# Converting float64 weights to float32: the absolute value scaled on ScalarE instead of a maximum on GpSimd or VectorE and a mask of bits

## The chip, the cores and the metric

The kernel runs on one core of a Trainium2 chip. The engines are named as in the profile: PE is TensorE (matmuls; PEld its weight loads), DVE is VectorE, ACT is ScalarE, POOL is GpSimd, SP is SyncE, from whose queue (SPq) nearly all DMA transfers are issued. The metric is the device time of one execution in microseconds; it is given as the median of several runs.

## The reference, cut to what matters

Eight batches of attention with eight heads, 576 positions, 64 values per head. The mask lets heads 0 to 3 see the 32 positions up to their own ("local") and heads 4 to 7 every 32nd position ("strided"). The output goes through a mix over positions of rank 32 and a feed-forward block. U, V, w_ch1 and w_ch2 arrive as float64.

```python
attn = softmax(where(mask, q @ k.T / 8, -1e9))         # per batch and head
x = concat_heads(attn @ v)                             # (8, 576, 512)
h = x.transpose(0, 2, 1) @ U @ V                       # rank 32
u = x + h.transpose(0, 2, 1)
out = u + np.maximum(u @ w_ch1, 0.0) @ w_ch2           # 512 -> 2048 -> 512
```

## The kernel before

The 4608 rows of u are worked through in 18 blocks of up to 256 rows. For each block `gemm1` (L625, sums in the PSUM tile `ph`) makes 128 of the 2048 hidden values at a time, and `gemm2` (L642, sums in `acc` or `px`) adds their share of the output. A float32 factor is held as two parts, hi and lo (`uh`/`ul`, `gh`/`gl`, `w[:, 0]`/`w[:, 1]`), and three products are made in place of one. Between the two products ACT makes `gh` (L629) and DVE makes `gl` (L630); a `gemm2` needs both, and each of them has three buffers.

The weights come in 32 chunks of 128 x 512. A chunk is loaded as 8-byte words (`raw`, L157, on SP's queue), converted to float32 in a tile `cv` by `to_f32` (L106 to L124), rounded to its hi part on ACT (L169) and subtracted from it on POOL for the lo part (L170). U and V go through `to_f32` too, as three smaller tiles. `to_f32` reads the high word of a float64 as if it were a float32, and its steps are:

- the absolute value on ACT (L115);
- the maximum with `TINY` (2 to the power -15), so that what is below float32's range does not wrap (L116). The argument `CMODE = (1, 1, 1, 0, 1, 1, 1, 0)` puts this step on POOL for three chunks of four and on DVE for the fourth; for U and V it is on DVE;
- a shift by three bits to the left together with an and-mask, on DVE (L118);
- an and/or with the high word on DVE, which brings back the sign and the top bit of the exponent (L120);
- a shift/or with the low word on DVE, for the last three bits (L122).

The first 90 us hold the attention of batch 0, staggered pair of heads by pair, its mix (L475 to L509, which makes u from x by way of `ta`, `tst` and V) and the transposes of the first blocks (L590 to L595); the conversions of the first chunks lie between them in the program. In that part a pair of heads goes through: transposes of q and k on PE (L203), copies of them out of PSUM on ACT into `kZ` and `qT` (L226), scores (L299), softmax (L322 to L325), a transpose of the weights (L330) and its copy `PT`, and the product with the values in `vt` or `vt_kept` (L340). `vt` and `vt_kept` hold the values twice, shifted by 32 rows; the second time is a copy on ACT (L226). Strided heads get their values by way of a DRAM tile `sd` and write their results `o_sb` to a DRAM tile `od`, from which they are loaded into `xg`, the tile of x.

After that the loop over blocks runs. Its first two blocks are worked through in turns, and the conversions of the remaining chunks lie between them, by the need of the next product or at 1.35 chunks for each step (`CONVM`). The attention of later batches fills the gaps of the later blocks.

The order on each engine's queue is not that of the program's text: the framework places each instruction by a modelled time line of its own, so that a change in an instruction's kind or count can move others. An engine runs its own queue strictly in that order.

Of the kernel before, what the change touches and what calls it, by code (L numbers as in the profile page):

```python
# [7 lines left out]
F32 = mybir.dt.float32  # L8
# [5 lines left out]
ALU = mybir.AluOpType  # L14
# [32 lines left out]
def fused_kernel(ctx, tc, q, k, v, U, V, w1_in, w2_in, masks, eye, out):  # L47
# [29 lines left out]
    banks = {"n": 0, "prefix": True}  # L77

    def psx2():
        """Two PSUM banks; those of the output sums serve too before the first of them."""  # L80
        banks["n"] += 1
        if banks["prefix"] and banks["n"] % 3 == 0:
            return ps_acc.tile([128, 2, 512], F32, name="acc")
        return ps_x.tile([128, 2, 512], F32, name="px")
# [18 lines left out]
    Vst = const.tile([96, S], F32R, name="Vst")  # L103
    raws, w_parts = {}, {}

    def to_f32(raw, p, n, eng=nc.vector, one=False):  # L106
        """float32 of float64 bits: the top 24 significant bits; below float32's range 0."""
        rv = raw.bitcast(I32).rearrange("p (n two) -> p n two", two=2)
        lo_w, hi_w = rv[:, 0:n, 0], rv[:, 0:n, 1]
        cv = att([128, 512], "cv")  # L110
        f = cv[0:p, 0:n]
        if one:
            eng.tensor_scalar(out=f, in0=hi_w.bitcast(F32), scalar1=TINY, scalar2=None, op0=ALU.abs_max)
        else:
            nc.scalar.activation(out=f, in_=hi_w.bitcast(F32), func=AF.Abs)  # L115
            eng.tensor_scalar(out=f, in0=f, scalar1=TINY, scalar2=None, op0=ALU.max)  # L116
        i = cv.bitcast(I32)[0:p, 0:n]
        nc.vector.tensor_scalar(out=i, in0=i, scalar1=3, scalar2=0x3FFFFFF8,  # L118
                                op0=ALU.logical_shift_left, op1=ALU.bitwise_and)
        nc.vector.scalar_tensor_tensor(out=i, in0=hi_w, scalar=-0x40000000, in1=i,  # L120
                                       op0=ALU.bitwise_and, op1=ALU.bitwise_or)
        nc.vector.scalar_tensor_tensor(out=i, in0=lo_w, scalar=29, in1=i,  # L122
                                       op0=ALU.logical_shift_right, op1=ALU.bitwise_or)
        return f  # L124
# [35 lines left out]
    def weights():  # L160
        for n, (i, g, t) in enumerate(chunks):
            while wl["n"] <= n:
                next(wl["gen"])
                wl["n"] += 1
            f = to_f32(raws[i, g, t], 128, 512, *((nc.vector, False), (nc.gpsimd, False), (nc.vector, True), (nc.gpsimd, True))[CMODE[n % 8]])
            parts = const.tile([128, 2, 512], F32R, name=f"w{i}_{g}_{t}", tag=f"w{i}_{g}_{t}")
            w_parts[i, g, t] = parts
            hi, lo = parts[:, 0], parts[:, 1]
            nc.scalar.copy(out=hi, in_=f)  # L169
            nc.gpsimd.tensor_tensor(out=lo, in0=f, in1=hi.bitcast(F32), op=ALU.subtract)  # L170
            yield
# [24 lines left out]
        return xn  # L196

    def transpose_natural(dsts, xn, strided, engines):
        """dst[d, position] per head of load_natural, the positions class by class when strided."""
        tp = psx2().rearrange("p a x -> p (a x)")  # L200
        for t in range(5):
            n = 128 if t < 4 else 64
# [30 lines left out]
    vts = []  # L233

    def acquire(names):
        """The first of these buffers that no other part of the program is filling or reading, when one is free."""
        while True:
            for name in names:
                if name not in held:
                    held[name] = True  # L240
                    return name
            yield

    def value_tiles():
        """Values of two heads, each in its half of the rows and of the columns; what stays is written once."""
        for vt in (big([128, NCH, 2, D + 1], "vt"), const.tile([128, NCH, 2, D + 1], F32, name="vt_kept")):
            nc.gpsimd.memset(vt, 0.0)
            for hh in range(2):
                nc.gpsimd.memset(vt[64 * hh:64 * hh + 64, :, hh, D:D + 1], 1.0)
            vts.append(vt)  # L250

    def attention_pair(b, pr, sd, od, last):
        """Two heads of a batch: 32 positions attend to themselves and to the 32 before, in the order of the
        positions (local heads) or class by class (strided heads)."""
        strided = pr >= 2
        early = b < NSP
        pi = 4 * b + pr if early else None
# [125 lines left out]
            yield  # L383

    def strided_heads(b):
        """The strided heads of a batch: partition (head, class), 18 positions in each class."""
        st = big([128, 2 * NCH * D], "st")
        sq, sk = (st[:, x * NCH * D:(x + 1) * NCH * D].rearrange("p (i d) -> p i d", d=D) for x in range(2))

# [76 lines left out]
        return xgs[b], tails[b // 2]  # L466

    def mix_t(b, half):
        """tst[:, half] = hi, lo, hi parts of U^T x."""
        xg, xt = x_tiles(b)  # L470
        tb = 64 * (b % 2)
        cs = slice(256 * half, 256 * half + 256)
# [103 lines left out]
    uT = {}  # L576

    def transposes(n):
        """Halves of u^T of a block: DVE transposes blocks of 32 x 32, DMA carries each to its quarter of the partitions."""
        def parts():  # L580
            uT[n] = [ubuf([128, 2, 4, NDC, 32], name, F32R) for name in ("uh", "ul")]
            return uT[n]
# [88 lines left out]
            counts["conv"] += 1  # L671

    def needed(item):
        """Chunks of weights for gemm1 of this block and part of FF, and for gemm2 of those before."""
        return len(chunks) if item[0] >= NLEAD else 8 * (item[1] // FPG) + 4 + item[1] % FPG

    gen, nb, done = None, 1, 0
# [107 lines left out]
```

## Time and profile before

| what | value |
|---|---|
| time, median of 3 runs | 1019.03 us (1016.57 to 1020.28) |
| span of the profiled execution, first to last instruction | 1016.9 us |
| PE busy | 958.7 us (94%) |
| DVE busy | 648.8 us (64%) |
| POOL busy | 406.1 us (40%) |
| ACT busy | 313.0 us (31%) |

The profiled execution has no time of its own beside its span; the span lies 2.1 us below the median of the runs and inside their range. Busy times are those in which an engine executes an instruction; starts are in microseconds from the first instruction.

### The profile page before, as it was taken

The page shows a single profiled execution, that of the slowest core. Times are in us where ns is not written, and L with a number is a line of the kernel's source. Part 1 is how long each engine was busy: PE and PEld are TensorE (multiplying, and loading weights), DVE is VectorE, ACT ScalarE, POOL GpSimd, SP SyncE. Part 2 cuts the span into 40 slices and gives each one's busy share as a digit, 9 for nine tenths or more (in the row PEclk, how much of TensorE's full clock was granted, in tenths as well). Part 3 has the DMA queues.
Part 4 walks back from the last instruction along what each step waited for, and adds up shares of the span by engine and source line. Part 5 has one row for each costly group of instructions (what it writes and reads, how often), then busy time and mean ns, then how long its engine had stood idle before and what let it go on. Part 6 is the DMA issues. An engine that isn't in the chain of part 4 may idle for free.

```text
span 1016.9 us, 18249 instructions
## 1 busy us (share of the span) xinstructions
PE 958.7 (94%) x7164; PEld 832.6 (82%) x7164; DVE 648.8 (64%) x1184; ACT 313.0 (31%) x691; POOL 406.1 (40%) x397
## 2 busy tenths in 40 slices
PE   4576889999999999999999999999999999999997
PEld 2345678898898889978889888988898889999996
DVE  3567998979786868634768686968686864312121
ACT  6777545213311241111422133123321242111110
POOL 1324966965383429201447353735383410000000
PEclk9797999999999999999999999999999999999999
DMA  7865913042523250401252425052514200101000
GB/s 189 221 164 143 366 39 67 2 109 48 91 42 68 48 90 22 88 1 42 47 91 43 68 47 91 21 89 48 91 39 71 47 22 21 42 1 43 1 21 21
DMA packets 186094, 71.33 MB, mean 70 GB/s; under 512 B 148952, under 2 KB 177272, under 8 KB 186008
## 3 DMA queue, kind: packets, MB, share of 16 engines
q1 hardware_dynamic: 186008, 70.16, 32.4%
q8 instruction: 56, 0.92, 0.4%
q14 instruction: 30, 0.25, 0.1%
HBM read 51.64 MB, written 11.80 MB: 62 GB/s over the span
## 4 chain that ended last, share of the span: by engine, by line
PE 76%; DVE 7%; SPq 5%; POOL 4%; issue 3%; DMA 3%; ACT 2%; DVEq 0%; POOLq 0%; ACTq 0%
PE ph L625 35%; PE acc L642 33%; SPq L94 4%; POOL tmp L409 3%; PE px L299 2%; PE px L340 1%; DVE cv L120 1%; DVE st L439 1%; PE px L330 1%; POOL w L170 1%; SPq L157 1%; DVE cv L122 1%; PE px L475 1%; DMA raw<-in_moe_w_ch_dram 1%; PE px L501 1%
## 5 line engine op out<-in xcount | busy, mean ns | idle before, releaser
L625 PE MATMUL ph<-uh,w 128*128 128x256 f32 x2304 | 472.6, 286 | 8.1 <-DVE gl L630 7.3
L625 PEld LDWEIGHTS ph<-uh,w 128*128 128x128 f32 x2304 | 379.3, 190 | 29.4 <-DVE gl L630 11.9
L642 PE MATMUL acc<-w,gh 128*128 128x512 f32 x1088 | 341.5, 393 | 0.0
L625 PE MATMUL ph<-ul,w 128*128 128x256 f32 x1152 | 331.5, 288 | 1.6 <-DVE ul L595 1.6
L630 DVE SCALAR_TENSOR_TENSOR gl<-ph,gh 128x256 fp32r<-128x256 f32 x288 | 120.6, 419 | 244.9 <-ACT gh L629 243.5
L629 ACT ACTIVATE gh<-ph 128x256 fp32r<-128x256 f32 x288 | 110.3, 384 | 504.9 <-PE ph L625 452.8
L437 POOL TENSOR_TENSOR tmp<-st,s_st 128x448 f32<-128x448 f32 (+7 forms) x162 | 144.2, 912 | 237.2 <-DVE st L439 148.7
L625 PEld LDWEIGHTS ph<-ul,w 128*128 128x128 f32 x1152 | 217.3, 189 | 11.4 <-DVE ul L595 1.8
L642 PEld LDWEIGHTS acc<-w,gh 128*128 128x128 f32 x1088 | 194.3, 188 | 31.2 <-issue 2.2
L642 PE MATMUL acc<-w,gl 128*128 128x512 f32 x544 | 213.2, 392 | 0.2 <-DVE gl L630 0.2
L409 POOL TENSOR_TENSOR tmp<-st 128x576 f32<-128x576 f32 (+6 forms) x162 | 169.4, 1089 | 74.9 <-DMA st<-in_k_dram 29.2
L439 DVE TENSOR_REDUCE st<-tmp 128x64 f32<-128x64 f32 (+8 forms) x162 | 138.3, 873 | 4.4 <-POOL tmp L437 3.4
L642 PEld LDWEIGHTS acc<-w,gl 128*128 128x128 f32 x544 | 102.2, 188 | 19.3 <-issue 1.1
L411 DVE TENSOR_REDUCE s_st<-tmp 128x9 f32<-128x576 f32 (+6 forms) x162 | 87.8, 564 | 14.2 <-POOL tmp L409 13.6
L170 POOL TENSOR_TENSOR w<-cv,w 128x512 fp32r<-128x512 f32 x32 | 45.3, 1424 | 49.1 <-ACT w L169 46.9
L116 POOL TENSOR_SCALAR cv<-cv 128x512 f32<-128x512 f32 x24 | 40.0, 1670 | 42.2 <-ACT cv L115 36.8
L454 ACT COPY xg<-st 32x256 f32<-32x256 f32 x96 | 38.7, 404 | 37.3 <-DVE st L439 36.4
L299 PE MATMUL px<-kZ,qT 128*32 128x128 f32 x612 | 30.5, 303 | 8.5 <-ACT qT L226 8.4
L299 PEld LDWEIGHTS px<-kZ,qT 128*32 128x32 f32 x612 | 20.4, 120 | 18.3 <-ACT qT L226 9.9
L169 ACT CAST w<-cv 128x512 fp32r<-128x512 f32 x32 | 19.7, 618 | 44.0 <-DVE cv L122 37.4
L612 DVE TENSOR_TENSOR ul<-u,uh 128x1024 fp32r<-128x1024 f32 x15 | 21.9, 1460 | 14.3 <-ACT uh L611 14.3
L120 DVE SCALAR_TENSOR_TENSOR cv<-raw,cv 128x512 int32<-128x512 int32 x32 | 28.3, 888 | 0.4
(123 smaller groups left out, 686.6 us busy)
## 6 DMA issues: line engine op xcount, KB each, us to landing
raw<-in_moe_w_ch_dram SPq DMA_DIRECT2D x32, 512.0 KB, 8.0
out_dram<-xg SPq DMA_DIRECT2D x32, 256.0 KB, 2.2
u<-bt SPq DMA_DIRECT2D x240, 32.0 KB, 1.9
vt_kept<-in_v_dram SPq DMA_DIRECT2D x28, 144.0 KB, 3.6
st<-in_q_dram SPq DMA_DIRECT2D x24, 144.0 KB, 3.4
st<-in_k_dram SPq DMA_DIRECT2D x24, 144.0 KB, 4.8
st<-in_v_dram SPq DMA_DIRECT2D x24, 144.0 KB, 3.2
xn<-in_k_dram SPq DMA_DIRECT2D x48, 72.0 KB, 2.4
```

The costliest lines, as they stand in the source:

```text
L94: last_dma[0] = nc.sync.dma_start(out=out, in_=in_).ins
L116: eng.tensor_scalar(out=f, in0=f, scalar1=TINY, scalar2=None, op0=ALU.max)
L170: nc.gpsimd.tensor_tensor(out=lo, in0=f, in1=hi.bitcast(F32), op=ALU.subtract)
L299: nc.tensor.matmul(sp[32 * c4:32 * c4 + 32, t], qT[:, 32 * c:32 * c + 32], kZ[:, :, 32 * c:32 * c + 64], start=not early, stop=True, skip_ ...
L409: nc.gpsimd.tensor_tensor(out=tmp[:, 0:n], in0=sk[:, j0:j0 + n], in1=sq[:, i:i + 1].broadcast_to([128, n, D]), op=ALU.mult)
L411: late.append(lambda tmp=tmp, n=n, i=i, j0=j0: nc.vector.tensor_reduce(out=s_st[:, i, j0:j0 + n], in_=tmp[:, 0:n], axis=AX.X, op=ALU.add))
L437: nc.gpsimd.tensor_tensor(out=tv, in0=sv[:, 0:i + 1, d0:d0 + step], in1=s_st[:, i, 0:i + 1].broadcast_to([128, i + 1, step]), op=ALU.mult)
L439: late.append(lambda tv=tv, i=i, d0=d0, step=step: nc.vector.tensor_reduce(out=o_st[:, i, d0:d0 + step], in_=tv.rearrange("p j d -> p d j" ...
L625: nc.tensor.matmul(ph[:, 0:W], w_parts[0, g, dc][:, part, fs], ut[:, :, :, dc, :], start=(dc == 0 and i == 0), stop=(dc == NDC - 1 and i = ...
L629: nc.scalar.activation(out=gh[:, 0:W], in_=ph[:, 0:W], func=AF.Relu)
L630: nc.vector.scalar_tensor_tensor(out=gl[:, 0:W], in0=ph[:, 0:W], scalar=0.0, in1=gh[:, 0:W].bitcast(F32), op0=ALU.max, op1=ALU.subtract)
L642: nc.tensor.matmul(accs[n][:, s, :], gt[:, cs], w_parts[1, g, f][:, part, :], start=(fc == 0 and i == 0), stop=(fc == NFC - 1 and i == 2))
```

## The change

`to_f32` takes the absolute value on ACT with a scale of 2 to the power -112. That subtracts 112 from the 8 exponent bits which the float32 reading has, which is 896 in the 11 bits of float64, the difference of the two formats' biases; a value below the range becomes 0. After it the shift by three bits needs no mask, and the and-mask of the next step takes the sign alone. The maximum is gone, on POOL and on DVE, and with it the argument that placed it. Docstrings are removed in other functions and nothing else changes. All later lines have a number lower by 4: L118 becomes L115, L120 L116, L122 L118, L169 L165, L226 L222, L484 L480, L595 L591, L630 L626.

```diff
-    def to_f32(raw, p, n, eng=nc.vector, one=False):
-        """float32 of float64 bits: the top 24 significant bits; below float32's range 0."""
+    def to_f32(raw, p, n):
...
         f = cv[0:p, 0:n]
-        if one:
-            eng.tensor_scalar(out=f, in0=hi_w.bitcast(F32), scalar1=TINY, scalar2=None, op0=ALU.abs_max)
-        else:
-            nc.scalar.activation(out=f, in_=hi_w.bitcast(F32), func=AF.Abs)
-            eng.tensor_scalar(out=f, in0=f, scalar1=TINY, scalar2=None, op0=ALU.max)
+        nc.scalar.activation(out=f, in_=hi_w.bitcast(F32), func=AF.Abs, scale=2.0 ** -112)
         i = cv.bitcast(I32)[0:p, 0:n]
-        nc.vector.tensor_scalar(out=i, in0=i, scalar1=3, scalar2=0x3FFFFFF8,
-                                op0=ALU.logical_shift_left, op1=ALU.bitwise_and)
-        nc.vector.scalar_tensor_tensor(out=i, in0=hi_w, scalar=-0x40000000, in1=i,
+        nc.vector.tensor_scalar(out=i, in0=i, scalar1=3, scalar2=None, op0=ALU.logical_shift_left)
+        nc.vector.scalar_tensor_tensor(out=i, in0=hi_w, scalar=-0x80000000, in1=i,
                                        op0=ALU.bitwise_and, op1=ALU.bitwise_or)
...
-            f = to_f32(raws[i, g, t], 128, 512, *((nc.vector, False), (nc.gpsimd, False), (nc.vector, True), (nc.gpsimd, True))[CMODE[n % 8]])
+            f = to_f32(raws[i, g, t], 128, 512)
```

The framework's placing moves instructions of the first 140 us. Three places follow; a row is a line, an operation, the tile written and the tiles read, the shape, and how many in a row.

ACT's queue during the staggered pairs of batch 0, from the cast of the first chunk's hi part on (at 30.78 us in the profile before). Before:

```order
L169 CAST w_0_0_257<-cv 128x512
L226 COPY kZ<-acc 64x18x16 x4
L226 COPY PT<-px 128x640
L115 ACTIVATE cv<-raw_0_1_270 128x512
L226 COPY vt<-vt 32x17x64
L226 COPY qT<-px 64x18x16 x4
L226 COPY vt<-vt 32x17x64
L115 ACTIVATE cv<-raw_0_2_316 128x512
L226 COPY vt_kept<-vt_kept 32x17x64 x2
L169 CAST w_0_1_334<-cv 128x512
```

and with the change:

```order
L165 CAST w_0_0_253<-cv 128x512
L222 COPY kZ<-acc 64x18x16 x4
L222 COPY PT<-px 128x640
L113 ACTIVATE cv<-raw_0_1_266 128x512
L222 COPY qT<-px 64x18x16 x4
L222 COPY vt<-vt 32x17x64 x2
L165 CAST w_0_1_329<-cv 128x512
L113 ACTIVATE cv<-raw_0_2_312 128x512
L222 COPY vt_kept<-vt_kept 32x17x64
L222 COPY kZ<-px 64x288 x4
```

The four copies of a strided pair's `qT` stood behind the copy inside `vt`, and stand ahead of it now; the cast of the second chunk moved up too.

ACT's queue later in the same part, from the four copies of the last strided pair's `kZ` on (63.12 us in the profile before). Before:

```order
L226 COPY kZ<-acc 64x18x16 x4
L226 COPY qT<-px 64x18x16 x4
L325 ACTIVATE s_sb<-s_sb 128x640
L169 CAST w_0_0_587<-cv 128x512
L484 COPY ta<-ph 32x256
L115 ACTIVATE cv<-raw_0_1_471 128x512
L226 COPY vt_kept<-vt_kept 32x17x64
L226 COPY PT<-px 128x640
L484 COPY ta<-ph 32x256
```

and with the change:

```order
L222 COPY kZ<-acc 64x18x16 x4
L321 ACTIVATE s_sb<-s_sb 128x640
L165 CAST w_0_0_579<-cv 128x512
L222 COPY vt_kept<-vt_kept 32x17x64
L222 COPY qT<-px 64x18x16 x4
L222 COPY vt_kept<-vt_kept 32x17x64
L480 COPY ta<-ph 32x256
L113 ACTIVATE cv<-raw_0_1_465 128x512
L222 COPY PT<-px 128x640
L480 COPY ta<-ph 32x256
```

A copy inside `vt_kept` stood behind the first `ta`; now it stands ahead of the four copies of `qT`, and a second one ahead of the first `ta`.

DVE's queue in the loop over blocks, before from the third `gl` on (105.70 us in the profile before), with the change the last twelve rows up to the fourth and fifth `gl`. Before:

```order
L630 SCALAR_TENSOR_TENSOR gl<-ph,gh 128x256
L120 SCALAR_TENSOR_TENSOR cv<-raw_1_3_861,cv 128x512
L118 TENSOR_SCALAR cv<-cv 128x512
L120 SCALAR_TENSOR_TENSOR cv<-raw_1_2_810,cv 128x512
L595 TENSOR_TENSOR ul<-px,uh 128x4x4x32
L122 SCALAR_TENSOR_TENSOR cv<-raw_1_3_861,cv 128x512
L120 SCALAR_TENSOR_TENSOR cv<-raw_1_0_958,cv 128x512
L122 SCALAR_TENSOR_TENSOR cv<-raw_1_2_810,cv 128x512
L122 SCALAR_TENSOR_TENSOR cv<-raw_1_0_958,cv 128x512
L118 TENSOR_SCALAR cv<-cv 128x512
L630 SCALAR_TENSOR_TENSOR gl<-ph,gh 128x256 x2
```

and with the change:

```order
L115 TENSOR_SCALAR cv<-cv 128x512
L118 SCALAR_TENSOR_TENSOR cv<-raw_1_0_947,cv 128x512
L116 SCALAR_TENSOR_TENSOR cv<-raw_1_1_968,cv 128x512
L116 SCALAR_TENSOR_TENSOR cv<-raw_1_2_970,cv 128x512
L118 SCALAR_TENSOR_TENSOR cv<-raw_1_1_968,cv 128x512
L118 SCALAR_TENSOR_TENSOR cv<-raw_1_2_970,cv 128x512
L115 TENSOR_SCALAR cv<-cv 128x512 x2
L116 SCALAR_TENSOR_TENSOR cv<-raw_1_3_972,cv 128x512
L116 SCALAR_TENSOR_TENSOR cv<-raw_2_0_974,cv 128x512
L115 TENSOR_SCALAR cv<-cv 128x512
L118 SCALAR_TENSOR_TENSOR cv<-raw_1_3_972,cv 128x512
L626 SCALAR_TENSOR_TENSOR gl<-ph,gh 128x256 x2
```

The third `gl` stands eight rows ahead of this piece. Between the third and the fourth `gl` there were 8 conversion steps (L118, L120, L122); there are 17 now (L115, L116, L118), in both cases with one `ul`, and now with one copy of `qT`.

## Rows read from the trace of the kernel before

**Rows 1.** The page: the engines' busy time (share of the span, instructions); PE's granted clock in tenths of full speed, in 40 slices of the span; and the maximum's group on POOL (line, engine, operation, tiles, shapes, count; busy us, mean ns of one; idle before).

```profile
PE 958.7 (94%) x7164; PEld 832.6 (82%) x7164; DVE 648.8 (64%) x1184; ACT 313.0 (31%) x691; POOL 406.1 (40%) x397
...
PEclk9797999999999999999999999999999999999999
...
L116 POOL TENSOR_SCALAR cv<-cv 128x512 f32<-128x512 f32 x24 | 40.0, 1670 | 42.2 <-ACT cv L115 36.8
```

**Rows 2.** Stretches of the span. Columns: stretch, length, then busy time (and instructions) of PE, PEld, DVE, ACT and POOL, PE's granted clock, share of the DMA engines, GB/s.

```profile
30.00:60.00 30.00, 16.80 (x211) 12.45 (x213) 14.39 (x33) 22.95 (x38) 8.31 (x6) 0.72 0.70 171
60.00:98.00 38.00, 23.59 (x300) 16.97 (x293) 26.88 (x55) 30.44 (x49) 11.37 (x9) 0.83 0.61 153
98.00:140.00 42.00, 34.77 (x243) 28.90 (x243) 39.54 (x54) 21.90 (x43) 37.10 (x24) 1.00 0.64 250
115.00:137.00 22.00, 17.71 (x107) 14.71 (x107) 21.90 (x29) 8.89 (x19) 18.77 (x13) 1.00 0.46 185
140.00:240.00 100.00, 98.06 (x724) 86.30 (x723) 88.11 (x160) 30.11 (x66) 70.85 (x64) 1.00 0.28 55
240.00:1017.00 777.00, 770.28 (x5558) 677.65 (x5556) 468.13 (x859) 189.32 (x468) 272.25 (x285) 1.00 0.27 49
```

**Rows 3.** List of groups on DVE from 0 to 240 us with shapes kept apart: the maximum where it is on DVE.

```profile
L116 DVE TENSOR_SCALAR cv<-cv 128x512 f32<-128x512 f32 x8 | 5.4, 680 | 7.2 <-ACT cv L115 7.2
```

**Rows 4.** Time line of ACT (start, duration, what, count, idle before and its releaser) at the two places shown above.

```profile
34.14 0.69 ACT L226 COPY PT<-px 128x640 f32<-128x640 f32 x1
34.73 0.67 ACT L115 ACTIVATE cv<-raw 128x512 f32<-128x512 f32 x1
37.18 1.10 ACT L226 COPY vt<-vt 32x1088 f32<-32x1088 f32 x1 [1.78 <-DMA vt<-sd]
38.19 2.68 ACT L226 COPY qT<-px 64x288 f32<-64x288 f32 x4
...
65.97 2.68 ACT L226 COPY qT<-px 64x288 f32<-64x288 f32 x4
68.68 0.74 ACT L325 ACTIVATE s_sb<-s_sb 128x640 f32<-128x640 f32 x1
...
69.95 0.36 ACT L484 COPY ta<-ph 32x256 f32<-32x256 f32 x1
```

**Rows 5.** Time line of PE: the same 36 products with the values at two times, the scores that wait for the first place on ACT, and the first product with V.

```profile
34.93 2.38 PE L340 MATMUL acc<-vt_kept,PT 128*32 128x130 f32 x36 [1.71 <-issue]
...
40.92 2.35 PE L299 MATMUL px<-kZ,qT 128*32 128x128 f32 x36 [2.96 <-ACT qT L226]
...
59.33 1.30 PE L340 MATMUL px<-vt_kept,PT 128*32 128x130 f32 x36 [0.54 <-ACT PT L226]
...
81.44 1.19 PE L501 MATMUL px<-tst,Vst 96*128 96x512 f32 x2 [0.95 <-DVE tst L491]
```

**Rows 6.** Time line of SP's queue from 59 to 67 us.

```profile
59.65 1.46 SPq L94 DMA_DIRECT2D xn<-in_q_dram  x2
61.23 3.15 SPq L94 DMA_DIRECT2D xg<-od  x4
...
65.89 0.92 SPq L94 DMA_DIRECT2D vt_kept<-sd  x2
```

**Rows 7.** Transfers issued from 55 to 72 us: those into `vt_kept`, KB each and median us from issue to landing.

```profile
vt_kept<-sd SPq DMA_DIRECT2D x2, 144.0 KB, 5.2
```

**Rows 8.** Time line of DVE: the last piece of the last strided pair's result, the stretch from the third `gl` to the fifth, and two later shifts.

```profile
95.83 0.28 DVE L369 TENSOR_TENSOR o_sb<-px,rt 64x128 f32<-64x128 f32 x1
...
105.70 0.41 DVE L630 SCALAR_TENSOR_TENSOR gl<-ph,gh 128x256 fp32r<-128x256 f32 x1
...
106.64 1.51 DVE L118 TENSOR_SCALAR cv<-cv 128x512 int32<-128x512 int32 x1
108.07 1.77 DVE L120 SCALAR_TENSOR_TENSOR cv<-raw,cv 128x512 int32<-128x512 int32 x1
109.77 0.68 DVE L595 TENSOR_TENSOR ul<-px,uh 128x512 fp32r<-128x512 f32 x1
110.37 0.68 DVE L122 SCALAR_TENSOR_TENSOR cv<-raw,cv 128x512 int32<-128x512 int32 x1
...
114.62 0.74 DVE L630 SCALAR_TENSOR_TENSOR gl<-ph,gh 128x256 fp32r<-128x256 f32 x2
...
119.70 0.83 DVE L118 TENSOR_SCALAR cv<-cv 128x512 int32<-128x512 int32 x1
...
141.37 0.42 DVE L118 TENSOR_SCALAR cv<-cv 128x512 int32<-128x512 int32 x1
```

**Rows 9.** Time line of POOL over the same stretch.

```profile
106.22 3.08 POOL L170 TENSOR_TENSOR w<-cv,w 128x512 fp32r<-128x512 f32 x2
109.26 3.73 POOL L116 TENSOR_SCALAR cv<-cv 128x512 f32<-128x512 f32 x2
112.96 4.58 POOL L170 TENSOR_TENSOR w<-cv,w 128x512 fp32r<-128x512 f32 x3
117.50 3.62 POOL L116 TENSOR_SCALAR cv<-cv 128x512 f32<-128x512 f32 x2
```

**Rows 10.** What PE waited for from 98 to 140 us (first row), and from 140 us to the end (second row): line waited at, releaser, us in total, times, longest.

```profile
PE ph L625 <- DVE gl L630: 5.0, 5, 1.5
...
PE ph L625 <- DVE gl L630: 2.3, 3, 1.1
```

## Prediction

> **What bounds the kernel now.** I read the page's engines first, then stretches of the span, then what PE waits for, and last the time lines of the engines at which PE waits. PE is busy for 94% of the span [rows 1], and the stretches tell where the other 6% lie [rows 2]. From 240 us on PE works 770.28 of 777 us, and from 140 to 240 us 98.06 of 100. From 98 to 140 us it works 34.77 of 42 and so stands for 7.2 us, 4.3 of them from 115 to 137 us (17.71 of 22). Ahead of 98 us it is busy for little more than half the time, at a mean granted clock of 0.72 and 0.83. So what the change can win or lose lies before 140 us; after it every delay of PE is handed on to the end one for one, and idle time of DVE or POOL is worth nothing. From 98 to 140 us DVE is busy for 39.54 of 42 us and POOL for 37.10 [rows 2], and PE waits there for `gl` from DVE, 5.0 us in 5 waits [rows 10]; another 2.3 us of such waits follow after 140 us. DVE, with the conversions in its queue, sets the pace of this stretch; the attention of batch 0 sets that of the first 98 us.
>
> **The change part by part.** *Removed.* 24 maxima on POOL, 40.0 us at 1.67 each [rows 1], and 8 on DVE, 5.4 us at 0.68 [rows 3], besides three on smaller tiles, under 2 us together at that price. PE waits directly for none of them. *Changed in kind.* The absolute value gets a scale. An exponential with a scale on 640 columns takes 0.74 us and a plain copy of as many 0.69 [rows 4], so I put the scale at nothing; at the other end it is 0.05 us for each of 32, 1.6 us on an engine that is idle for two thirds of the span. The shift loses its mask: with it one takes 0.42 us undisturbed [rows 8], as much as the `gl` of half the columns, and no row shows one alone; I take 0.42 too, and from zero to 0.2 us less as its bounds. The rest of the sum is order.
>
> *First place on ACT.* The copy inside `vt` waits 1.78 us for its transfer, and the copies of `qT` (2.68 us) stand behind it until 40.87 us [rows 4]. Ahead of it they start when the absolute value ends, 34.73 + 0.67 = 35.4 us, and end at 38.1: 2.8 us gained. The conversions queued on DVE ahead of them lose a maximum of 0.68 us [rows 3], which I count as 0.7 more. PE's scores, which wait 2.96 us for `qT` [rows 5], start at 37.4 in place of 40.92: **-3.5 us**. That gain travels down to the loads of `xg` from `od`, issued at 61.23 us [rows 6], which move to about 57.5.
>
> *Second place on ACT.* It takes this back. A copy inside `vt_kept` stands ahead of the last `qT` now, and waits for a load that SP issued at 65.89 us behind 3.15 us of `xg` loads [rows 6]. With those earlier by 3.7 us, less the `xn` loads (1.46 us) that stood ahead of them and now come between, it is issued at about 63.4 and lands 5.2 us later [rows 7], at 68.6. Behind it come the copy (1.1), `qT` (2.68, ends at 72.4 where it ended at 68.65), and a second copy (1.1): `ta` starts at about 73.5 where it started at 69.95 [rows 4]. One of the two copies lay between the two `ta` before, so of these 3.55 us some 1.1 come back by the second `ta`. PE's first product with V, at 81.44 us [rows 5], comes **+2.4 us** late. Hidden behind this stands the gain of the first place: if the load of `vt_kept` landed 3 to 4 us sooner, it would be kept.
>
> *Into the loop.* DVE does two steps of 0.6 us less between the two `ul`, so the last piece of `o_sb`, at 95.83 us [rows 8], after which SP's queue is free for the weights, is late by 2.4 - 1.2 = **+1.2**. ACT then has five absolute values in a row ahead of the second `gh`, where three stood between the first and the third, spread out: 2 x 0.67 = 1.3 us. The third `gl` comes at 105.70 + 1.2 + 1.3 = 108.2.
>
> *DVE's queue.* From the third to the fourth `gl` took 114.62 - 105.70 = 8.9 us, for 8 conversion steps. Undisturbed, a step with two tensors is followed by the next 0.60 us later (109.77 to 110.37 [rows 8]), a shift takes 0.42, a `gl` 0.34 to the next start: 6 x 0.60 + 2 x 0.42 + 0.60 (`ul`) + 0.34 = 5.4. The other 3.5 us are stretching. A shift takes 1.51 and an and/or 1.77 at 106.64 and 108.07, while POOL subtracts at 106.22 [rows 8, 9]. Beside POOL's maxima (109.26 and 117.50) a step with two tensors takes 0.68 as it does alone, and a shift 0.83. With the change 17 steps lie there: 12 x 0.60 + 5 x 0.42 + 0.60 + 0.46 (`qT`) + 0.34 = 10.7 us. Their stretching: none if no subtraction falls on them; at most two thirds of the time of six subtractions of 1.54 us, 6 us. I take 3.3, since the subtractions stay and it is near to what the same place shows now. The fourth `gl` comes at 108.2 + 10.7 + 3.3 = 122.2, **+7.6 us**, and PE, with only three buffers of `gl`, stands until then.
>
> The exchange is that more chunks are done by then: 19 by the fourth `gl` in place of 16, so that the following `gl` have almost no conversion ahead of them. The 4.3 us that PE idles from 115 to 137 us go, and the 17.7 us of work in that stretch are done at 122.2 + 17.7 = 139.9 instead of 137: **+2.9**. Of the later waits (2.3 us [rows 10]) I take **-1.0**, by the same lead in chunks. The sum is +1.9 on a span of 1016.9, 1018.8; the median of the runs lies 2.1 above the profiled span, which gives **1021 us**. By the bounds of the stretching alone it is 1017.6 to 1023.6.
>
> **The rivals.** *Faster: POOL's maxima were what stretched DVE.* Then the waits for DVE from 98 to 140 us go with them: at most the 7.2 us that PE stands there, 1019 - 7.2 = 1012. For it: both engines are busy nearly all the time there, and a shift takes 0.83 us instead of 0.42 beside a maximum (119.70 [rows 8]). Against it: the long stretches lie beside subtractions, which stay, and a step with two tensors is not lengthened beside a maximum. The Trainium skill, SBUF — State Buffer, section "Who interferes with whom", says that DVE and GpSimd share one pair of ports as an exclusive lock: a two-tensor step on DVE contends with any GpSimd instruction that reads SBUF, and a fast-mode tensor_scalar is blocked for the whole of it. By that rule the maxima would block DVE as the subtractions do and this rival would hold; the 1.51 us shift agrees with it, the 0.68 us of the step at 110.37 beside a maximum do not.
>
> *Faster: the gain of the first place is kept*, since the load of `vt_kept` lands in time. Then PE is 6 us earlier at 81 us (-3.5 instead of +2.4), all later times move with it, and the time is 1015, on the edge of what can be told from no change.
>
> *Slower: the clock.* PE does little before 98 us, and its mean granted clock there is 0.72 over 30 us and 0.83 over 38 [rows 2]; at the lower of its two levels (1.2 instead of 2.4 GHz) 36 products take 2.38 us, against 1.30 [rows 5]. A mean of 0.83 over 38 us is 13 us at half speed. The forecast's pause ahead of the fourth `gl` is longer than any that PE has after 98 us now; if the clock falls in it and stays low for 10 to 13 us, 5 to 6.5 us more are lost, 1026 to 1027. From 6.4 us at the low level on (3.2 us lost) it decides, since 1021 becomes more than 1024.1; against it stands the granted clock of 1.00 from 98 to 140 us, idle times and all. *Slower: the stretching doubles*, because more subtractions now fall between the third and the fourth `gl`, and the later `gl` wait too: 6 us more, 1027.
>
> *It does not do what it says*: the scheduler's moves cancel and nothing on PE's path moves, 1019.
>
> **How the numbers follow.** A change under 0.5% (5.1 us) can hardly be told from none for this kernel, so the bounds are 1013.9 and 1024.1. The sum 0.33, nothing moves 0.07, the first place's gain kept 0.14 (half below 1013.9), POOL's maxima stretched DVE 0.17, clock 0.17, stretching doubles 0.12. Faster is 0.17 + 0.07 = 0.24, same 0.33 + 0.07 + 0.07 = 0.47, slower 0.17 + 0.12 = 0.29. The range goes from 1011, just past the first rival, to 1028, past the two slow ones.
>
> **What would show it.** Right: PE's scores near 37.4 us; `ta` later than 72 us; the fourth `gl` between 120 and 124 us with PE idle ahead of it; no waits for `gl` from there to 140 us; PE busy to the end with an unchanged amount of work. Wrong: a granted clock under 1.0 after 98 us; `vt_kept` copies that do not wait; shifts and two-tensor steps at 0.42 and 0.6 us all through the stretch (the ports), or a fourth `gl` before 116 us.

## The result, and the profile after

The changed kernel takes 1027.11 us (1025.66 to 1028.49, 4 runs), the kernel before 1018.89 over its 4 runs: a ratio of 1.0076 (95% interval 1.0055 to 1.0096). It is slower by 0.8%, inside the range of the forecast and outside what it held likeliest. The span grew by 7.5 us, from 1016.9 to 1024.4.

The page after, engines and PE's granted clock, to be read against [rows 1]:

```profile
PE 965.5 (94%) x7164; PEld 837.5 (82%) x7164; DVE 639.1 (62%) x1173; ACT 313.2 (31%) x691; POOL 366.4 (36%) x373
...
PEclk8778899999999999999999999999999999999999
```

PE issues the same 7164 products and is busy 6.8 us longer; its idle time grew by 0.7 us only. It took longer for the same products, and the granted clock is lower (a mean of 0.972 over the span, 0.985 before). The stretches (columns as in [rows 2]) tell where:

```profile
107.83:120.64 12.81, 9.78 (x41) 8.29 (x41) 12.75 (x15) 5.78 (x11) 6.55 (x6) 0.77 1.02 412
120.64:124.47 3.83, 3.15 (x10) 2.13 (x10) 3.83 (x7) 2.52 (x5) 1.35 (x1) 0.57 0.88 349
...
98.00:140.00 42.00, 30.51 (x178) 24.45 (x177) 39.56 (x54) 23.27 (x44) 19.54 (x13) 0.88 0.63 246
140.00:240.00 100.00, 98.55 (x728) 86.17 (x729) 80.29 (x150) 29.69 (x65) 58.16 (x55) 1.00 0.28 55
240.00:1024.00 784.00, 777.61 (x5607) 684.34 (x5605) 470.04 (x865) 189.83 (x471) 272.29 (x286) 1.00 0.27 49
```

From 140 us on PE works 98.55 + 777.61 = 876.16 us, against 98.06 + 770.28 = 868.34 before [rows 2]: at 140 us it has 7.8 us more work ahead of it, and that is the whole loss. From 98 to 140 us it was busy for 30.51 us instead of 34.77, part of that at the lower level of the clock (0.77 from 107.83 us, 0.57 from 120.64), where it was 1.00 before.

The places that the prediction named, time line of ACT:

```profile
34.62 2.75 ACT L222 COPY qT<-px 64x288 f32<-64x288 f32 x4
...
66.85 1.10 ACT L222 COPY vt_kept<-vt_kept 32x1088 f32<-32x1088 f32 x1 [1.85 <-DMA vt_kept<-sd]
68.51 2.66 ACT L222 COPY qT<-px 64x288 f32<-64x288 f32 x4 [0.55 <-PE px L199]
...
72.34 0.36 ACT L480 COPY ta<-ph 32x256 f32<-32x256 f32 x1
```

`qT` starts at 34.62 instead of 38.19, the copy inside `vt_kept` waits 1.85 us for its load, and `ta` comes at 72.34 instead of 69.95 [rows 4]. Time line of PE:

```profile
37.42 1.28 PE L295 MATMUL px<-kZ,qT 128*32 128x128 f32 x36 [1.50 <-ACT qT L222]
...
82.99 1.22 PE L497 MATMUL px<-tst,Vst 96*128 96x512 f32 x2
...
106.19 0.36 PE L621 MATMUL ph<-uh,w 128*128 128x256 f32 x1 [4.46 <-DVE gl L626]
107.83 0.58 PE L621 MATMUL ph<-uh,w 128*128 128x256 f32 x1 [1.29 <-DVE gl L626]
...
110.56 1.05 PE L638 MATMUL acc<-w,gh 128*128 128x512 f32 x2
...
120.64 1.22 PE L638 MATMUL px<-w,gh 128*128 128x512 f32 x2 [3.03 <-ACT gh L625]
...
124.47 0.39 PE L621 MATMUL ph<-uh,w 128*128 128x256 f32 x1 [0.68 <-DVE gl L626]
```

The scores start at 37.42 (40.92 [rows 5]) and the product with V at 82.99 (81.44). From 101.7 us on, behind the transposes of a block, PE then stands 4.46 us and 1.29 us for a `gl`, and 3.03 us for a `gh` (L638 is `gemm2`, L621 `gemm1`). Time line of DVE:

```profile
105.62 0.43 DVE L626 SCALAR_TENSOR_TENSOR gl<-ph,gh 128x256 fp32r<-128x256 f32 x1
...
107.37 0.41 DVE L626 SCALAR_TENSOR_TENSOR gl<-ph,gh 128x256 fp32r<-128x256 f32 x1
...
109.16 0.46 DVE L224 COPY qT<-acc 64x288 f32<-64x288 f32 x1
...
124.00 0.74 DVE L626 SCALAR_TENSOR_TENSOR gl<-ph,gh 128x256 fp32r<-128x256 f32 x2
```

The third `gl` comes at 107.37 (105.70 [rows 8]) and the fourth at 124.00 (114.62): 9.4 us late. DVE has no idle time between the two. What PE waited for from 98 to 140 us, and from 140 us on (last row), against [rows 10]:

```profile
PE ph L621 <- DVE gl L626: 7.3, 4, 4.5
PE px L638 <- ACT gh L625: 3.0, 1, 3.0
...
PE ph L621 <- DVE gl L626: 3.8, 4, 1.3
```

### The profile page after: what moved, and what is told of

It is laid out like the page before. It is cut to its first block, busy times and chain, and to the rows that moved or that the text cites. A ratio compares the mean times of both kernels' runs of the same rounds, so it can differ in the third digit from the quotient of the medians.

```text
span 1024.4 us, 18207 instructions
## 1 busy us (share of the span) xinstructions
PE 965.5 (94%) x7164; PEld 837.5 (82%) x7164; DVE 639.1 (62%) x1173; ACT 313.2 (31%) x691; POOL 366.4 (36%) x373
## 4 chain that ended last, share of the span: by engine, by line
PE 76%; DVE 10%; DMA 4%; ACT 4%; SPq 3%; issue 2%; POOL 1%; DVEq 0%; ACTq 0%; POOLq 0%
PE ph L621 35%; PE acc L638 32%; SPq L94 2%; PE px L295 2%; PE px L336 2%; DVE cv L116 2%; DMA raw<-in_moe_w_ch_dram 1%; PE px L638 1%; DVE cv L118 1%; DVE st L435 1%; DMA xn<-in_q_dram 1%; ACT qT L222 1%; DMA xn<-in_k_dram 1%; DVE gl L626 1%; ACT kZ L222 1%
## 5 line engine op out<-in xcount | busy, mean ns | idle before, releaser
L621 PE MATMUL ph<-uh,w 128*128 128x256 f32 x2304 | 472.7, 286 | 12.8 <-DVE gl L626 11.1
L621 PEld LDWEIGHTS ph<-uh,w 128*128 128x128 f32 x2304 | 379.0, 190 | 33.4 <-DVE gl L626 10.9
L638 PE MATMUL acc<-w,gh 128*128 128x512 f32 x1088 | 343.6, 395 | 0.0
L621 PE MATMUL ph<-ul,w 128*128 128x256 f32 x1152 | 331.2, 288 | 0.0
L626 DVE SCALAR_TENSOR_TENSOR gl<-ph,gh 128x256 fp32r<-128x256 f32 x288 | 120.3, 418 | 240.2 <-ACT gh L625 239.0
L621 PEld LDWEIGHTS ph<-ul,w 128*128 128x128 f32 x1152 | 217.1, 188 | 9.8 <-issue 0.2
L638 PEld LDWEIGHTS acc<-w,gh 128*128 128x128 f32 x1088 | 195.8, 189 | 31.5 <-issue 2.0
L638 PE MATMUL acc<-w,gl 128*128 128x512 f32 x544 | 213.7, 393 | 0.0
L638 PEld LDWEIGHTS acc<-w,gl 128*128 128x128 f32 x544 | 102.5, 188 | 18.9 <-issue 1.3
L115 DVE TENSOR_SCALAR cv<-cv 128x512 int32<-128x512 int32 (+3 forms) x35 | 21.7, 634 | 19.0 <-ACT cv L113 19.0
L165 ACT CAST w<-cv 128x512 fp32r<-128x512 f32 x32 | 19.7, 618 | 32.9 <-DVE cv L118 31.0
L116 DVE SCALAR_TENSOR_TENSOR cv<-raw,cv 128x512 int32<-128x512 int32 x32 | 29.0, 919 | 0.3
```

What stands on the lines that cost most here:

```text
L116: nc.vector.scalar_tensor_tensor(out=i, in0=hi_w, scalar=-0x80000000, in1=i, op0=ALU.bitwise_and, op1=ALU.bitwise_or)
L621: nc.tensor.matmul(ph[:, 0:W], w_parts[0, g, dc][:, part, fs], ut[:, :, :, dc, :], start=(dc == 0 and i == 0), stop=(dc == NDC - 1 and i = ...
L626: nc.vector.scalar_tensor_tensor(out=gl[:, 0:W], in0=ph[:, 0:W], scalar=0.0, in1=gh[:, 0:W].bitcast(F32), op0=ALU.max, op1=ALU.subtract)
L638: nc.tensor.matmul(accs[n][:, s, :], gt[:, cs], w_parts[1, g, f][:, part, :], start=(fc == 0 and i == 0), stop=(fc == NFC - 1 and i == 2))
```

## The experiments

Theory Q: the loss lies in the order that the framework's scheduler chose, not in the instructions. Rivals: the new forms cost something (I), or the clock falls for another reason (C). To hold the order apart from the instructions, a table with the queue of every engine is added, and an edge from each instruction to the next in that table:

```diff
     finish(len(blocks) - 1)
+    per = {}
+    for ins in nc.cur_bb.bb.instructions:
+        if type(ins).__name__ != "BassTilePoolBoundary":
+            per.setdefault(str(ins.engine).split(".")[-1], []).append(ins)
+    for e, spans in ORDER.items():
+        ranks = [r for a, n in spans for r in range(a, a + n)]
...
+        for a, b in zip(ranks, ranks[1:]):
+                tc.add_manual_dep(per[e][b], per[e][a].name, mybir.DependencyInfo(
+                    mybir.DependencyClass.NoSync, mybir.DependencyReason.DATA), reason="order")
```

The edges make no wait; they fix the place in the queue. Runs with this table differ from each other only in it, unless said. Their lines have numbers higher by 8 than the changed kernel's (L646 is `gemm2`, L629 `gemm1`, L634 `gl`, L633 `gh`), and by 10 where maxima are put back ahead of them. Ratios are to the kernel before on the same chip; the sets of runs lie on several chips, so that between sets the ratios compare better than the times.

**The changed kernel in the order of before.** `ORDER` holds the queues of the kernel before, without the maxima.

> The changed kernel's instructions, each engine's queue put by added ordering edges into the order that the kernel before has (without the maxima). Theory Q (the loss is the order that the scheduler chose: conversion steps ahead of the second and fourth gl on DVE and gh on ACT): the loss goes, and since DVE does 2.7 us less from 98 to 140 us and POOL 18 us less there, 1010 to 1019 us; fourth gl at 108 to 115 us, PE at a granted clock near 1.0 from 98 us on. Theory I (the new forms cost something themselves: the scaled absolute value, the shift without a mask): 1024 to 1028 us in spite of the order. Theory C (the clock falls for a reason that has nothing to do with the order): 1022 to 1028 us with half speed after 98 us.

1013.18 us, ratio 0.9955 (0.9943 to 0.9967); a second time, on another chip, 1013.27 us, 0.9950 (0.9934 to 0.9966).

> The changed kernel's instructions in the order of before once more, as the measure for the three runs beside it on the same chip: 1012 to 1015 us, ratio 0.994 to 0.997.

**The maxima put back, the order left to the scheduler.**

```diff
         nc.scalar.activation(out=f, in_=hi_w.bitcast(F32), func=AF.Abs, scale=2.0 ** -112)
+        eng.tensor_scalar(out=f, in0=f, scalar1=0.0, scalar2=None, op0=ALU.max)
```

> The changed kernel with the maximum put back behind the scaled absolute value, on the engine that had it (against zero, so it changes no value); the scheduler then chooses exactly the order of the kernel before on all engines. Theory Q: as before, 1017 to 1021 us. Theory I: 1024 to 1028 us. Theory C: 1022 to 1028 us. Against the first run of this set it prices the maxima themselves at an equal order: Q expects them to be worth 0 to 9 us.

1018.88 us, ratio 1.0009 (0.9997 to 1.0021): as before. So the scaled absolute value and the unmasked shift cost nothing that can be told (at most 0.2%), and I falls. No run shows what becomes of a value below float32's range. At one and the same order the maxima are worth 1018.9 - 1013.2 = 5.7 us. The changed order costs 1027.1 - 1013.2 = 13.9 us by the times and 1.0076 - 0.9955 = 1.2%, 12.3 us, by the ratios: the change wins the one and loses the other. The engines' busy time on the page of the first of the two runs in the order of before:

```profile
PE 962.7 (95%) x7164; PEld 837.0 (83%) x7164; DVE 637.0 (63%) x1173; ACT 312.6 (31%) x691; POOL 364.5 (36%) x373
```

and its stretches, columns as in [rows 2]:

```profile
0.00:98.00 98.00, 59.92 (x646) 42.55 (x647) 50.78 (x108) 71.68 (x115) 15.92 (x19) 0.74 0.69 174
98.00:140.00 42.00, 38.49 (x263) 33.38 (x262) 37.94 (x56) 22.46 (x45) 18.52 (x14) 0.95 0.64 249
```

From 98 to 140 us PE is busy for 38.49 us (30.51 in the changed kernel). C in its strong form falls too: this run has more time at the low clock than the kernel before (PE busy 962.7 against 958.7 us for the same products; 0.74 in the first 98 us), and is faster.

**Which part of the order.** One run takes the changed kernel's queues up to the first `gh` and `gl`, and those of before for the rest; the other the reverse.

> The changed kernel's instructions; up to the first gh and gl (some 96 us) the queues stand as in the changed kernel, and all that is left as in the kernel before. Theory Q, loss in the loop: 1010 to 1020 us, within 3 us of the run in the order of before. If instead the first 98 us cost the time (copies inside vt_kept, PE at half speed there): 1024 to 1028 us.

> The changed kernel's instructions; up to the first gh and gl the queues stand as in the kernel before, and all that is left as in the changed kernel. Theory Q, loss in the loop: 1023 to 1029 us, like the changed kernel, with the fourth gl 16 to 18 us behind the third and PE standing ahead of it. If the first 98 us cost the time: 1010 to 1020 us.

1014.75 us (0.9967, 0.9954 to 0.9979) and 1026.18 us (1.0083, 1.0069 to 1.0097). The order of the loop costs 11 to 13 us (1.0076 - 0.9967 and 1.0083 - 0.9955), that of the first 98 us at most one or two, which the intervals do not tell from nothing. These two runs also take the clock out: over their runs the mean granted clock is 0.975 with the loop of before and 0.974 with that of the changed kernel, and their times are 11.4 us apart.

**Mending DVE and ACT in the changed order.** The prediction had named DVE's queue. Three runs move `gl` and `gh` up in the changed kernel's order and leave PE's queue alone. The first moves the second and third:

```diff
 L222 COPY qT
+L625 gh (second)
 L113 x2
+L625 gh (third)
 L113 x3
-L625 gh x2
```

> The changed kernel in its own order with two places mended: on ACT the second and third gh ahead of the run of five absolute values, on DVE the second gl ahead of all nine conversion steps that stood before it and the third behind three of them. Theory Q1 (the 17 steps ahead of the fourth gl alone set the time, and PE's 4.5 us wait for the second gl only comes earlier than a wait that it would meet anyway): 1024 to 1028 us, fourth gl still at 121 to 124 us. Theory Q2 (each wait of PE for a gl is paid for by itself): 1020 to 1023 us. Theory C (PE's half speed from 106 to 117 us, set off by that 4.5 us pause, is what costs): 1020 to 1023 us with full speed there.

The second moves the fourth and fifth, the third run all four:

> The changed kernel in its own order with two other places mended: on ACT the fourth gh ahead of the casts that wait for DVE's conversions and the fifth behind three of these, on DVE the fourth gl behind 8 of the 17 conversion steps and the fifth behind 12. Theory Q1: fourth gl at about 112, fifth at about 117 us, PE's 3.0 us wait for gh and the 0.7 us behind it gone, and 1.7 us of half speed with them: 1021 to 1024 us. Theory Q2 says nearly the same, 1022 to 1024. Theory C: the half speed from 106 us on stays, 1025 to 1028 us.

> Both mendings of the two runs before this one together, nothing else. Theory Q1 and Q2: the loss of the loop is in these four places, so the time comes near the run in the order of before, 1012 to 1018 us. If the rest of the changed order costs as much (the order of the casts, of the chunks, of PE's products): 1019 to 1024 us.

1026.14 us (ratio 1.0062, 1.0048 to 1.0077), 1032.77 (1.0118, 1.0100 to 1.0136) and 1029.68 (1.0096, 1.0076 to 1.0115). The first has the time that Q1 expected, with the fourth `gl` at 126.12 us where it put 121 to 124; its clock stayed low (0.78 from 98 to 140 us), so that it could not try C. The other two are misses: the fourth `gl` did come earlier, at 119.09 and 116.51 us instead of 124.00, and the time rose. In the run that moved the second and third, PE's time line shows that the wait only changes its name, from `gl` to `uh`, and that the one for `gh` is longer:

```profile
107.61 0.79 PE L629 MATMUL ph<-uh,w 128*128 128x256 f32 x2 [3.31 <-ACT uh L598]
...
122.76 1.22 PE L646 MATMUL px<-w,gh 128*128 128x512 f32 x2 [5.06 <-ACT gh L633]
```

In the run with all four, PE's time line still has its first `gemm2` at 109.26 us, and a wait of 3.41 us for a `gh`:

```profile
109.26 1.19 PE L646 MATMUL acc<-w,gh 128*128 128x512 f32 x2 [0.96 <-DVE qT L232]
...
121.61 1.22 PE L646 MATMUL acc<-w,gh 128*128 128x512 f32 x2 [3.41 <-ACT gh L633]
```

and DVE's time line shows it standing 4.04 us for a `gh`, where it had no idle time in the changed kernel; ACT's time line shows that this `gh` in turn waits 4.40 us for PE's sums:

```profile
116.51 0.42 DVE L634 SCALAR_TENSOR_TENSOR gl<-ph,gh 128x256 fp32r<-128x256 f32 x1 [4.04 <-ACT gh L633]
```

```profile
116.09 0.39 ACT L633 ACTIVATE gh<-ph 128x256 fp32r<-128x256 f32 x1 [4.40 <-PE ph L629]
```

So an instruction moved up in DVE's queue stands for ACT's, and that one for PE's.

One thing that all these runs share is what PE's queue holds. In the kernel before, the first product of `gemm2` stands behind 24 products of `gemm1`, which is two calls of 12; with the change it stands behind 49, four calls and the first product of a fifth. `ph` has two buffers, so a fourth `gemm1` must wait for the second `gl` and a fifth for the third (PE's waits of 4.46 and 1.29 us above), and the first `gemm2` stands behind both. In the changed kernel `acc` is not free earlier either, since the last `qT` is copied out of it at 109.16 us (in the run with all four, PE's wait of 0.96 us is for that copy); but the run with the first part of before has the copy at 97.74 us and is as slow. The first `gemm2` in the time line of PE of the kernel before:

```profile
100.61 0.71 PE L642 MATMUL acc<-w,gh 128*128 128x512 f32 x2
```

in the changed kernel's instructions in that order:

```profile
100.60 0.71 PE L646 MATMUL acc<-w,gh 128*128 128x512 f32 x2
```

and with the first part of before and the loop of the changed kernel, with PE's wait ahead of it:

```profile
107.15 0.36 PE L629 MATMUL ph<-uh,w 128*128 128x256 f32 x1 [3.52 <-DVE gl L634]
...
111.46 1.05 PE L646 MATMUL acc<-w,gh 128*128 128x512 f32 x2
```

In all runs with the loop of before it lies at 99.0 to 103.2 us and the time at 1011.8 to 1019.8 us; in all with the loop of the changed kernel at 109.3 to 112.9 us, and the time at 1026.1 to 1032.8. PE's queue was not moved by itself, so this is a common mark of the slow runs, and not shown to be the cause; among the slow runs it does not go with the time (109.26 us and 1029.68, 110.79 us and 1026.14). DVE's queue has a common mark too, since the three runs moved no `gl` from the sixth on: counted on DVE's time line, 58 or 59 conversion steps of 128x512 stand ahead of the sixth `gl` in all five runs with the loop of the changed kernel, and 45 in all nine with that of before. By 140 us DVE has started 6 to 8 `gl` in the first and 11 in the second. Which queue of the loop costs how much stays open.

**The price of the maxima, engine by engine.** In the order of before, with the maxima of one engine put back in their old places:

> The changed kernel's instructions in the order of the kernel before, with the 24 maxima on POOL put back in their old places (against zero, so they change no value) and the 8 on DVE and those of the three small tiles left out. If the removed work was worth something because POOL's maxima lengthen the chain of a chunk and block steps of DVE: 1016 to 1019 us. If it was worth something because DVE, which is busy all the time from 98 to 140 us, has 8 steps less: 1013 to 1015 us.

> The counterpart: the maxima on DVE put back in their old places (8 chunks and the three small tiles), those on POOL left out. POOL's maxima as the cause: 1013 to 1015 us. DVE's steps as the cause: 1016 to 1019 us. If both runs of this pair lie between, near 1016, the two shares add up.

POOL's alone give 1017.42 us (0.9988, 0.9977 to 0.9998), DVE's alone 1014.60 (0.9959, 0.9944 to 0.9973), none 1013.27 on the same chip. So POOL's maxima cost 4.2 us, and those on DVE 1.3, which the intervals do not tell from nothing. Groups of DVE from 0 to 240 us without maxima (shift/or, and/or, shift; columns as in [rows 3]):

```profile
L126 DVE SCALAR_TENSOR_TENSOR cv<-raw,cv 128x512 int32<-128x512 int32 x32 | 26.9, 847 | 0.3
L124 DVE SCALAR_TENSOR_TENSOR cv<-raw,cv 128x512 int32<-128x512 int32 x32 | 25.0, 785 | 0.4
L123 DVE TENSOR_SCALAR cv<-cv 128x512 int32<-128x512 int32 x32 | 22.0, 693 | 6.7 <-ACT cv L121 6.6
```

and with POOL's maxima:

```profile
L128 DVE SCALAR_TENSOR_TENSOR cv<-raw,cv 128x512 int32<-128x512 int32 x32 | 29.6, 932 | 0.3
L126 DVE SCALAR_TENSOR_TENSOR cv<-raw,cv 128x512 int32<-128x512 int32 x32 | 27.8, 874 | 0.4
L125 DVE TENSOR_SCALAR cv<-cv 128x512 int32<-128x512 int32 x32 | 25.0, 789 | 6.7 <-ACT cv L121 4.7 <-POOL cv L123 1.8
```

The same steps take 85, 89 and 96 ns longer on average, 82.4 - 73.9 = 8.5 us over the 96 of them. POOL's time line near the fourth `gl`, without maxima:

```profile
104.51 2.73 POOL L174 TENSOR_TENSOR w<-cv,w 128x512 fp32r<-128x512 f32 x2 [6.43 <-ACT w L173]
111.31 1.61 POOL L174 TENSOR_TENSOR w<-cv,w 128x512 fp32r<-128x512 f32 x1 [4.08 <-ACT w L173]
```

and with them:

```profile
107.75 3.74 POOL L123 TENSOR_SCALAR cv<-cv 128x512 f32<-128x512 f32 x2
111.46 4.58 POOL L176 TENSOR_TENSOR w<-cv,w 128x512 fp32r<-128x512 f32 x3
```

With the maxima the subtractions queue up at this place and run three in a row (4.58 us) beside DVE's steps. A maximum also stretches steps by itself: a shift takes 0.83 us beside one [rows 8]. How the 8.5 us divide between these two effects is not shown.

**The first place's gain.** The changed kernel's queues up to 58 us, and those of before from there on; then the same with two `xn` loads ahead of the `xg` loads on SP's queue, as before:

> The changed kernel's instructions; the queues stand as in the changed kernel up to some 58 us (qT ahead of the copy inside vt, xg loads ahead of the xn loads), and from there on as in the kernel before (ta and the last qT ahead of the copies inside vt_kept). The prediction's rival that the first place's gain is kept: 3 to 4 us below the run in the order of before, 1009 to 1011 us. If a later wait takes the gain (loads of xn, DVE): 1012 to 1014 us.

> As the run that kept the first place's gain, with one thing different: on SP's queue the two xn loads of the last strided pair stand ahead of the xg loads, as in the kernel before. In that run PE waited 2.6 us for these xn, and only 0.6 us of the 3.5 us reached the second gl. If that wait is what took the gain: 1 to 2 us below the run in the order of before, 1010.5 to 1012.5 us, second gl near 98.5 us. If the xg loads, now later, take it instead: 1013 to 1014 us.

1013.55 us (0.9937, 0.9921 to 0.9954) and 1011.78 us (0.9934, 0.9920 to 0.9948). PE's time line of the first:

```profile
37.33 2.35 PE L303 MATMUL px<-kZ,qT 128*32 128x128 f32 x36 [0.16 <-ACT qT L230]
...
63.59 1.05 PE L207 MATMUL px<-ident,xn 128*128 128x128 f32 x4 [2.59 <-DMA xn<-in_q_dram]
```

The scores keep their gain (37.33 us), and 26 us later PE waits 2.59 us for `xn`. With `xn` ahead the second `gl` is another 0.5 us earlier, and by the ratios the two runs are the same. The last run has the lowest time of all, 7.0 us below the kernel before on the same chip; against the plain order of before (1013.27) its gain of 1.5 us is about as large as the interval. On PE's time lines the first product with V starts at 80.64 us in the order of before, at 80.00 with the first place alone, and at 83.85 in the run with the changed kernel's queues up to the first `gh`, which has both places: the first place gains 0.6 us there, and the second, with what else moved between 58 us and the first `gh`, costs 3.9.

## Why the prediction was right or wrong

*Direction and range.* The range held; the likeliest value, 1021, was 6 us low, and "same", held likeliest, was wrong. The range reaches to 1028 for two slow rivals with 0.29 between them, so it holds by them and not by the sum.

*First and second place.* The times are right: 37.42 us was forecast as 37.4, the `xg` loads go out at 56.45 (57.5), `ta` at 72.34 (73.5), V at 82.99 (83.8). (The load of `vt_kept` "at about 63.4" is 63.7 by its own terms; nothing hangs on it.) The rival that the first place's gain is kept was priced at 6 us at V. Without the second place V comes 3.9 us earlier (80.00 against 83.85), and the times then lie 1.2 us apart, 0.3% by the ratios (0.9937 against 0.9967). The rest of the 6 us was not to be had: of the first place's gain only 0.6 us reaches V even so, and with the loads of `xn` ahead another 0.5. What takes the rest is not shown.

*Fourth `gl`.* Nearly right: 124.00 against 122.2, +9.4 instead of +7.6. The third `gl` came 0.8 us earlier than forecast; from it to the fourth are 16.6 us, 5.9 more than the 10.7 of undisturbed steps, where the sum took 3.3. That DVE's 17 steps fill this time is right, as DVE does not stand in it. That PE stands for it is right in part: it waited for `gh` and 0.68 us for `gl` there, and moving the `gl` ahead of most of the steps won nothing.

*The step that failed* is the next one: "so that the following `gl` have almost no conversion ahead of them. The 4.3 us that PE idles from 115 to 137 us go", and with it the -1.0 on later waits. I expected 5.7 us to come back after the fourth `gl`; 9.4 - 7.5 = 1.9 came. From the fourth `gl` to the end, before:

```profile
114.62:1016.90 902.28, 889.04 (x6432) 781.16 (x6432) 580.21 (x1051) 229.94 (x554) 365.26 (x363) 1.00 0.28 53
```

and with the change, the first 16 us apart too:

```profile
124.00:140.00 16.00, 13.50 (x98) 10.60 (x98) 16.00 (x22) 6.59 (x12) 9.44 (x6) 1.00 0.02 7
124.00:1024.40 900.40, 889.66 (x6432) 781.11 (x6432) 566.33 (x1035) 226.10 (x547) 339.88 (x347) 1.00 0.27 49
```

At the fourth `gl` PE has the same 6432 products left in each kernel, 889.04 and 889.66 us of work; PE's idle time from there on fell from 13.2 to 10.7 us only. The three chunks of lead were there, but not where they were expected to help: DVE stays busy for 16.00 of 16 us, and ahead of the sixth to ninth `gl` stand 7, 4, 4 and 3 conversion steps, 18 in place of 16 before (5, 4, 4, 3). The `gl` without conversions ahead of them are the tenth to twelfth, from 142.91 us on. PE still waited 3.8 us for `gl` after 140 us, more than the 2.3 of before [rows 10].

*Rival "the stretching doubles".* I gave it 0.12, and what it names is what the rows show: 5.9 us of stretching instead of 3.3, later `gl` waiting too, and the time at its 1027. POOL's time line from the third to the fourth `gl`:

```profile
105.63 2.94 POOL L166 TENSOR_TENSOR w<-cv,w 128x512 fp32r<-128x512 f32 x2 [10.51 <-ACT w L165]
112.27 2.78 POOL L166 TENSOR_TENSOR w<-cv,w 128x512 fp32r<-128x512 f32 x2 [3.69 <-ACT w L165]
116.33 1.61 POOL L166 TENSOR_TENSOR w<-cv,w 128x512 fp32r<-128x512 f32 x1 [1.28 <-ACT w L165]
119.23 2.76 POOL L166 TENSOR_TENSOR w<-cv,w 128x512 fp32r<-128x512 f32 x2 [1.28 <-ACT w L165]
```

POOL subtracts for 8.4 us of that time, against 4.7 before [rows 9], and for each of these DVE's steps are stretched by 0.7 us in both kernels (5.9 and 3.5 us). Of the 5.6 us by which the sum fell short of the span, 2.6 are this stretching, less the 0.8 of the third `gl`, and 3.8 are what did not come back.

*Rival "POOL's maxima stretched DVE".* I gave it 0.17 and argued that the stretching lies beside subtractions, which stay, and that a step with two tensors is not lengthened beside a maximum. The second was read from too few steps: the one at 123.20 us of the profile before takes 0.98 us beside a maximum. At an equal order the rival holds in kind: 4.2 us by POOL alone and 5.7 in all, against the 7.2 that I set as its most. The Trainium skill, SBUF — State Buffer, section "Who interferes with whom", has DVE and GpSimd share a pair of ports under an exclusive lock; the steps of 0.98 and 0.83 us beside a maximum, as those of 1.51 and 1.77 beside subtractions [rows 8], agree with it; the 0.68 us of the step at 110.37 beside a maximum do not.

*Rival "the clock".* It gives the number that came, 1026 to 1027, and the clock did fall after 98 us (0.88). But from 101 to 142 us DVE does not stand, so a faster PE would not have had a `gl` sooner: its slower work from 107.83 to 117 us lies ahead of the 3.03 us wait for `gh`, and that from 120.64 us on ahead of the 0.68 us wait for the fourth `gl`. The runs say the same: the two that exchange the loop lie 11.4 us apart at one mean clock, and the first mended run, at 0.78 from 98 to 140 us, ended 1 us ahead of the changed kernel. Over the 45 runs of the kernel before that were timed beside the experiments, a mean granted clock lower by 0.01 goes with 1.4 us more (95% interval 0.2 to 2.7). The changed kernel's is lower by 0.008 (0.969 against 0.977); by that, as an estimate, the clock costs some 1 us of the 8.

## What to carry to other kernels

Where a scheduler sets the order, removing instructions is two changes: the work that goes, and a new order. Price them apart, by pinning the old order and removing the work; here the first was worth 5.7 us and the second cost 12 to 14. When the new order is read ahead of a run, do not stop at the first late instruction: count, over the whole stretch in which the engine that bounds has to wait, what stands ahead of each instruction that it needs (45 conversion steps ahead of the sixth `gl` before, 59 with the change). And read the queues together: an instruction moved up in one of them can stand there for another queue, as `gl` did for 4.04 us.

## What was not expected of the hardware

The clock in the first 98 us matters little to the time. The kernel with the maxima put back has the order of before, and a mean granted clock of 0.77 there; the kernel before has 0.85. First 98 us of the kernel before, columns as in [rows 2]:

```profile
0.00:98.00 98.00, 55.62 (x646) 39.78 (x647) 53.02 (x113) 71.65 (x115) 25.85 (x26) 0.85 0.69 174
```

and with the maxima put back:

```profile
0.00:98.00 98.00, 59.63 (x657) 42.80 (x658) 54.59 (x115) 72.61 (x117) 27.39 (x27) 0.77 0.70 178
```

PE is busy for 4.0 us more in that stretch, and the profiled spans are 1015.5 and 1016.9 us. PE waits there for ACT, DVE and loads [rows 5], so slower products can fill its pauses. It is not quite nothing: from 140 us on the clock is full in both, a mean clock lower by 0.01 is 10 us of PE's work at full speed over the span, and the 45 runs above put 1.4 us on it, about a seventh.
